# Block-sparse attention followed by an FFN: row-tiled scores, a mask product on VectorE, channels-first AV, row sums on TensorE, and operands turned by transposing DMAs

## Chip, cores, metric

The kernel runs on one core of one Trainium2 chip. The metric is device microseconds (us) of one execution; a kernel's figure is the median of its runs. A run can fall into a slower state, with a lower granted clock (the share of full speed that TensorE's clock was allowed, as the trace records it) and a longer time. A profile is of one run; those of e1 and e9 are of runs 1.8 and 2.0 us above their medians, that of e3 of one 3.6 above, that of e6 of its fastest. A profiled execution lists the span from the first to the last instruction, which is about 2 us shorter than the execution's time.

## The reference

```python
# q, k, v: (4 batches, 8 heads, 768 positions, 64) float32
scores = (q @ k.transpose(0, 1, 3, 2)) / sqrt(64)
mask   = window of +-1 block of 32 | first/last block row/column | 3 sampled blocks per block row
attn   = softmax(where(mask, scores, -1e9))
x      = (attn @ v) as 3072 tokens x 512 channels
h      = x @ w_in                            # 512 -> 2048
out    = (h * sigmoid(beta * h)) @ w_out     # 2048 -> 512, float32
```

Both kernels compute all 768x768 scores of each head densely in fp16 with float32 accumulation and apply the mask to them. They use sigmoid(z) = (1 + tanh(z/2))/2, and no maximum is subtracted before exp.

## The kernel before

Two heads form a *pair*, of 128 channels. k, q and v of a pair are loaded as float32, cast on VectorE, turned by TensorE (`tp`) and evicted by VectorE into operands of up to 128 rows: 64 channels plus 24 rows (one for each block of 32 positions) that carry the mask as a product of block one-hots, so that one matmul gives masked scores. The FFN of a group of tokens is kept in a backlog of small pieces that are put between the attention steps of the next group.

```python
def emit_prep(b, j):                                   # cut
    for name, st32 in (("k", kst), ("q", qst)):
        nc.vector.tensor_copy(out=st16..., in_=st32...)          # cast
        for c in range(NC):                                      # NC = 6
            nc.tensor.transpose(out=tp[:, c, :], in_=st16[:, c, :, :]..., identity=identity)
        nc.vector.tensor_copy(out=four[f"{name}A"][0:D, :], in_=flat[0:D, :])
        nc.vector.tensor_copy(out=four[f"{name}B"][D:P, :], in_=flat[D:P, :])
    ...                                                # v is cast into va, beside a column of ones

def step(hh, kc0):                                     # scores of one head, cut
    for i in range(kn):
        nc.tensor.matmul(sc[:, i * n:(i + 1) * n],
                         lhsT=kx[0:rows, (kc0 + i) * P:(kc0 + i + 1) * P],   # rows = 88 or 128
                         rhs=qx[0:rows, q0:q0 + n], start=True, stop=True)
    nc.scalar.activation(out=et[:, 0:kn * n], in_=sc[:, 0:kn * n], func=AF.Exp, scale=SCALE)

def av_step(hh):                                       # tokens first, cut
    for qc in range(nq):
        for kc in range(NC):
            nc.tensor.matmul(av[:, qc, :], lhsT=et[...128 columns...],
                             rhs=va[:, hh, kc, 0:D + 1],         # 65th column: the row sum
                             start=(kc == 0), stop=(kc == NC - 1))
    nc.vector.reciprocal(out=recip[:, 0:nq], in_=av[:, 0:nq, D])
    nc.vector.tensor_tensor(out=xstage..., in0=av..., in1=recip..., op=ALU.mult)
    if hh == 1:
        ...                                            # xtp: turned by TensorE, evicted into xT_sb

def h_step(f):                                         # FFN, cut; both kernels have it
    for c in range(NPAIR):
        nc.tensor.matmul(hp[:, 0:n], lhsT=w_in_sb[:, c, f * P:(f + 1) * P], rhs=xT_sb[...], ...)
    nc.scalar.activation(out=t_sb, in_=hp, func=AF.Tanh, scale=beta_h_sb[:, f:f + 1])
    nc.vector.scalar_tensor_tensor(out=g[:, f, 0:n], in0=t_sb, scalar=1.0, in1=hp, ...)
def o_step(ts, quarter):
    ...                                                # 4 of 16 matmuls of op; after the last: osb, store
```

The softmax here doesn't subtract the row's maximum and nothing guards it: scores larger than these inputs give would overflow.

## Time and profile before

| before | |
|---|---|
| time | 339.36 us, median of 3 (339.35 to 339.81) |
| span of the profiled execution | 337.4 us |
| busy: TensorE (PE), ScalarE (ACT), VectorE (DVE) | 298.4, 215.8, 181.7 us |
| first score, first FFN matmul (hp), last score | 21.7, 52.7, 313.4 us |

The profile page first gives each engine's busy time, then the span in 40 equal slices with the busy share in tenths, then the chain of work that ended last, by engine. These are those lines of the page of the kernel before.

```profile
PE 298.4 (88%) x2659; PEld 172.2 (51%) x2659; DVE 181.7 (54%) x408; ACT 215.8 (64%) x297; POOL 28.0 (8%) x48
...
PE   0055589999999999999999999999999999999995
...
DMA  7999994112530340021340000011000010001101
...
PE 64%; DVE 16%; ACT 14%; issue 4%; DMA 2%; SPq 0%; ACTq 0%; DVEq 0%
```

After six slices (50 us) TensorE is busy nearly without a break, and the DMA engines, full at first, are idle most of the time. What bounds this kernel is the stream of matmuls, plus a start of about 50 us.

Groups of the page: line, engine, operation, output<-inputs, shape, count | busy us, mean ns of one | idle before, and what ended it.

```profile
L240 ACT ACTIVATE et<-sc 128x1024 f16<-128x1024 f32 (+1 forms) x160 | 146.8, 953 | 80.4 <-PE sc L234 80.2
L313 PE MATMUL op<-w_out_sb,g 128*128 128x512 f16 x384 | 97.0, 379 | 0.1
```

ScalarE waits 80 us for scores, so it is not the limit; `op` waits for nothing. The mean of 379 ns is a matmul from start to modelled end; from start to start one takes 216 ns.

**An account of TensorE's time.** I use one account for every kernel, worked out from the start times of the matmuls in the trace. Each matmul is charged its columns at 0.417 ns; tiles that run side by side are counted once ("stream"). Where the trace's record of the granted clock is 0.5 (half speed), and before its first record, where the spacings are twice as long as well, the extra time of the stream is put under "half clock". A gap of up to 150 ns between matmuls of different kinds is "change of kind", a longer one is a wait for whatever the trace names as having ended it. What remains is "other": waits for g or for transposes on TensorE, and some 3 ns per matmul. The expectations quoted below were written with an earlier form of it, in which the half clock was not kept apart and counted from other starting points, so their figures differ by some us from those here.

### The profile page before, as it was taken

How to read it: one execution, taken by the hardware profiler on the slowest of the kernel's cores; microseconds unless marked ns; L12 is line 12 of the kernel's file. 1: busy time of each engine (PE TensorE's matmuls, PEld its weight loads, DVE VectorE, ACT ScalarE, POOL GpSimd, SP SyncE). 2: the span in 40 equal slices, each digit the busy share in tenths (PEclk: the TensorE clock that was granted, in tenths of full speed). 3: DMA queues.
4: the chain of work that ended last, by engine and by line, in shares of the span. 5: the costliest groups of instructions: out<-in, count | busy, mean ns of one | idle time of the engine just before them, and what ended most of it. 6: DMA issues, size and time to landing. Idle time of an engine off the chain costs nothing.

```text
span 337.4 us, 6399 instructions
## 1 busy us (share of the span) xinstructions
PE 298.4 (88%) x2659; PEld 172.2 (51%) x2659; DVE 181.7 (54%) x408; ACT 215.8 (64%) x297; POOL 28.0 (8%) x48
## 2 busy tenths in 40 slices
PE   0055589999999999999999999999999999999995
PEld 0034466655555555555566445455455455555662
DVE  3989764543787451557866366115667114561360
ACT  1011389985998545978554989665986756954561
POOL 9994000000000000000000000000000000000000
PEclk9999999999999999999999999999999999999999
DMA  7999994112530340021340000011000010001101
GB/s 242 384 228 225 267 330 179 50 47 80 161 97 11 123 130 33 31 79 64 96 157 31 33 0 2 31 38 58 1 3 0 33 62 33 0 2 62 64 2 62
DMA packets 20880, 29.78 MB, mean 88 GB/s; under 512 B 1380, under 2 KB 17780, under 8 KB 20852
## 3 DMA queue, kind: packets, MB, share of 16 engines
q1 hardware_dynamic: 16512, 25.17, 21.8%
q0 software_dynamic: 4224, 4.19, 7.5%
q8 instruction: 21, 0.34, 0.4%
q14 instruction: 7, 0.06, 0.1%
q10 hardware_dynamic: 116, 0.01, 0.0%
HBM read 27.27 MB, written 6.29 MB: 99 GB/s over the span
## 4 chain that ended last, share of the span: by engine, by line
PE 64%; DVE 16%; ACT 14%; issue 4%; DMA 2%; SPq 0%; ACTq 0%; DVEq 0%
PE op L313 23%; PE hp L294 16%; PE sc L234 12%; PE av L260 9%; ACT et L240 8%; ACT t_sb L299 6%; DVE g L301 4%; PE tp L209 2%; PE xtp L274 2%; DMA qst<-in_q_dram 2%; DVE q_203 L204 1%; DVE va_70 L217 0%; DVE xst L266 0%; DVE qB_157 L214 0%; DVE qB_139 L214 0%
## 5 line engine op out<-in xcount | busy, mean ns | idle before, releaser
L240 ACT ACTIVATE et<-sc 128x1024 f16<-128x1024 f32 (+1 forms) x160 | 146.8, 953 | 80.4 <-PE sc L234 80.2
L313 PE MATMUL op<-w_out_sb,g 128*128 128x512 f16 x384 | 97.0, 379 | 0.1
L294 PE MATMUL hp<-xT_sb,w_in_sb 128*128 128x512 f16 (+1 forms) x448 | 95.6, 348 | 1.0 <-DVE g L301 0.2
L301 DVE SCALAR_TENSOR_TENSOR g<-t_sb,hp 128x512 f16<-128x512 f16 (+1 forms) x112 | 67.1, 610 | 44.9 <-ACT t_sb L299 44.4
L299 ACT ACTIVATE t_sb<-hp,beta_h_sb 128x512 f16<-128x512 f32 (+1 forms) x112 | 69.8, 653 | 12.1 <-PE hp L294 10.9
L294 PEld LDWEIGHTS <-w_in_sb 128*128 128x128 f16 x448 | 42.2, 97 | 35.9 <-issue 1.9
L260 PEld LDWEIGHTS <-et 128*128 128x128 f16 x1152 | 44.2, 99 | 21.6 <-DVE xst L266 10.4
L313 PEld LDWEIGHTS <-g 128*128 128x128 f16 x384 | 34.9, 97 | 33.2 <-DVE qB_163 L214 0.4
L265 DVE RECIPROCAL recip<-av 128x2 f32<-128x2 f32 (+1 forms) x64 | 11.2, 176 | 70.3 <-PE av L260 70.0
L318 ACT ACTIVATE osb<-op 128x512 f32<-128x512 f32 x24 | 14.3, 598 | 23.2 <-PE op L313 19.7
L266 DVE TENSOR_TENSOR xst<-av,recip 128x128 f16<-128x128 f32 (+1 forms) x64 | 22.8, 357 | 1.6
L276 DVE COPY xT_sb<-xtp 128x256 f16<-128x256 f16 (+1 forms) x32 | 11.5, 358 | 14.6 <-PE xtp L274 14.6
L274 PEld LDWEIGHTS <-xst 128*128 128x128 f16 x96 | 6.4, 97 | 12.5 <-DVE xst L266 12.2
L260 PE MATMUL av<-va_70,et 128*128 128x65 f16 x216 | 9.6, 199 | 2.8 <-DVE xst L266 2.7
L234 PE MATMUL sc<-qB_139,kB_138 128*128 128x256 f16 (+1 forms) x48 | 11.6, 344 | 0.5 <-ACT et L240 0.5
L274 PE MATMUL xtp<-identity,xst 128*128 128x128 f16 x96 | 10.9, 222 | 1.0 <-DVE xst L266 0.9
L234 PE MATMUL sc<-qA_137,kA_136 88*128 88x256 f16 (+1 forms) x48 | 11.1, 344 | 0.5 <-ACT et L240 0.3
L180 PE MATMUL mkx<-onehot,mask_121 24*24 24x512 f16 (+1 forms) x2 | 0.8, 506 | 10.3 <-DVE mask_121 L126 10.3
L260 PE MATMUL av<-va_72,et 128*128 128x65 f16 x216 | 9.5, 196 | 0.0
L234 PE MATMUL sc<-qB_145,kB_144 128*128 128x256 f16 (+1 forms) x36 | 8.8, 348 | 0.9 <-ACT et L240 0.9
L234 PE MATMUL sc<-qA_143,kA_142 88*128 88x256 f16 (+1 forms) x36 | 8.7, 350 | 0.6 <-ACT et L240 0.6
L234 PE MATMUL sc<-qB_163,kB_162 128*128 128x512 f16 (+1 forms) x36 | 8.5, 325 | 0.7 <-ACT et L240 0.7
(206 smaller groups left out, 249.4 us busy)
## 6 DMA issues: line engine op xcount, KB each, us to landing
kst<-in_k_dram SPq DMA_DIRECT2D x16, 384.0 KB, 4.7
qst<-in_q_dram SPq DMA_DIRECT2D x16, 384.0 KB, 5.5
vst<-in_v_dram SPq DMA_DIRECT2D x16, 384.0 KB, 5.4
out_dram<-osb SPq DMA_DIRECT2D x24, 256.0 KB, 2.0
w_in_sb<-in_moe_w_in_dram POOLq DMA_DIRECT2D x4, 512.0 KB, 10.1
w_out_sb<-in_moe_w_out_dram POOLq DMA_DIRECT2D x4, 512.0 KB, 21.7
sb_i_95<-in_sampled_blocks_dram ACTq DMA_DIRECT2D x1, 0.3 KB
beta_sb<-in_moe_beta_dram ACTq DMA_DIRECT2D x1, 8.0 KB, 4.5
```

Source lines behind the costliest of these rows:

```text
L234: nc.tensor.matmul(sc[:, i * n:(i + 1) * n], lhsT=kx[0:rows, (kc0 + i) * P:(kc0 + i + 1) * P], rhs=qx[0:rows, q0:q0 + n], start=True, stop ...
L240: nc.scalar.activation(out=et[:, 0:kn * n], in_=sc[:, 0:kn * n], func=AF.Exp, bias=0.0, scale=SCALE)
L260: nc.tensor.matmul(av[:, qc, :], lhsT=et[:, i * n + qc * P:i * n + (qc + 1) * P], rhs=va[:, hh, kc, 0:D + 1], start=(kc == 0), stop=(kc == ...
L265: nc.vector.reciprocal(out=recip[:, 0:nq], in_=av[:, 0:nq, D])
L266: nc.vector.tensor_tensor(out=xstage[:, 0:nq, hh * D:(hh + 1) * D], in0=av[:, 0:nq, 0:D], in1=recip[:, 0:nq].to_broadcast([P, nq, D]), op= ...
L274: nc.tensor.transpose(out=xtp[:, qc, :], in_=xstage[:, qc, :], identity=identity)
L276: nc.vector.tensor_copy(out=xT_sb[:, j, b * S + q0:b * S + q0 + n], in_=xtp[:, 0:nq, :].rearrange("p c s -> p (c s)"))
L294: nc.tensor.matmul(hp[:, 0:n], lhsT=w_in_sb[:, c, f * P:(f + 1) * P], rhs=xT_sb[:, c, t0:t0 + n], start=(c == 0), stop=(c == NPAIR - 1))
L299: nc.scalar.activation(out=t_sb[:, 0:n], in_=hp[:, 0:n], func=AF.Tanh, bias=0.0, scale=beta_h_sb[:, f:f + 1])
L301: nc.vector.scalar_tensor_tensor(out=g[:, f, 0:n], in0=t_sb[:, 0:n], scalar=1.0, in1=hp[:, 0:n], op0=ALU.add, op1=ALU.mult)
L313: nc.tensor.matmul(op, lhsT=g[:, f, ts * P:(ts + 1) * P], rhs=w_out_sb[:, f, :], start=(f == 0), stop=(f == N_FFC - 1))
L318: nc.scalar.activation(out=osb, in_=op, func=AF.Copy, bias=0.0, scale=0.5)
```

## The change

The intent is to take work off TensorE, which bounds the kernel.

- The scores of even and odd chunks of 128 keys run side by side in two row tiles of 64 rows (a row or column tile is a part of TensorE's 128x128 array that works on a matmul of its own; the way the array is cut is the tiling mode); the mask becomes a product with a 0/1 mask after exp, on VectorE.
- AV gives channels first (V as weights, exp moving), so that `xtp` and its eviction go; two heads run side by side in column tiles. Row sums become matmuls with ones, four tiles side by side. The reciprocal goes through DRAM and comes back spread over 64 partitions.
- k, q, v are cast by the loads (on GpSimd's queue) and turned by transposing DMAs (on SyncE's queue), so that `tp`, the casts and evictions go.
- The program order is fixed by hand, with lags in steps; `osb` moves from ScalarE to VectorE.

The core of the diff; setup, mask building, and the parts that only move are cut:

```diff
+    ctx.enter_context(tc.manual_schedule())
...
+    def emit_load(i):
+        for src, dst in ((k, k_stage[i % NST]), (q, q_stage[i % NST][:, 1:2 * NC + 1, :]), (v, va...)):
+            nc.gpsimd.dma_start(out=dst..., in_=src[b, 2 * j:2 * j + 2]...)       # casts to fp16
+    def emit_turn(i):
+        nc.sync.dma_start_transpose(out=kT, in_=k16.rearrange("p c d -> p (c d)"))
+        nc.sync.dma_start_transpose(out=qT[:, 1:2 * NC + 1:2, :], in_=q16[:, 1:2 * NC + 1, :]...)
+        nc.sync.dma_start_transpose(out=qT[:, 0:2 * NC + 1:2, :], in_=q16...)
...
-        nc.tensor.matmul(sc[:, i * n:(i + 1) * n], lhsT=kx[0:rows, ...], rhs=qx[0:rows, q0:q0 + n], ...)
+                for i, (hh, g) in enumerate(pieces):
+                    for par in range(2):
+                        nc.tensor.matmul(sc[:, par, i, :],
+                            lhsT=kT[par * D:(par + 1) * D, hh * (NC // 2) + g, :],
+                            rhs=qT[par * D:(par + 1) * D, lo:lo + nq, :], start=True, stop=True)
                 nc.scalar.activation(out=et, in_=sc, func=AF.Exp, bias=0.0, scale=SCALE)
+                nc.vector.tensor_tensor(out=et, in0=et, in1=mask_pg[...], op=ALU.mult)
...
+        def sums():
+            dt = av_pool.tile([P, 512], FP32, tag="av", name="dsum")     # av_pool has one buffer
+            ... for t in range(4):
+                    nc.tensor.matmul(dt[32 * t:32 * t + 32, 0:256],
+                        lhsT=sel[:, h, :] if nh == 2 else ones32,
+                        rhs=ets[(t // 2, t % 2, kc)][:, h * 256:(h + 1) * 256], ...)
+            nc.vector.reciprocal(out=r[...], in_=dt[...])                # twice, 128 columns
+            nc.sync.dma_start(out=dr, in_=r)                             # to DRAM
+            ... nc.sync.dma_start(out=rb[hh * D:(hh + 1) * D, 0:n], in_=src.to_broadcast([D, n]))
+        def av(jj):
+            at = av_pool.tile([P, 512], FP32, tag="av", name="av")
+            for kc in range(NC):
+                for hh in range(2):
+                    nc.tensor.matmul(at[hh * D:(hh + 1) * D, 0:n], lhsT=va[:, hh, kc, :],
+                                     rhs=ets[(jj, hh, kc)], ...)
+            nc.vector.tensor_tensor(out=xt[...], in0=at[:, 0:n], in1=box["rb"][jj][:, 0:n], op=ALU.mult)
...
+    for i in range(1, NPAIR):
+        emit_load(i)
+    for i in range(4):
+        emit_w_in(i)
+    for i in range(4):
+        emit_w_out(i)
+    LAG_S, LAG_A0, LAG_A1 = 2, 8, 9          # steps from a couple's last score to sums, av, av
+    PACE = 1.28                              # us of FFN work fed behind each score step
+    ... while n_turned < len(seq) and first_use[n_turned] <= x + 7: emit_turn(n_turned) ...
+        feed(PACE if x < n_steps else 1.0)
```

Steps are 144, one exp of 128x1024 each; a *couple* is two pairs of one block of 256 or 512 queries.

## The prediction

> **What bounds it now.** TensorE. Busy: PE 298 us of 337, ACT 216, DVE 182; the chain of waits is 64% PE. Start-to-start spacing in the timeline: 216 ns for a 512-column matmul (op: 32 in 6.92 us), about 39 ns for a 65-column av matmul. With these the PE stream is: hp 83, op 83, scores 62, av 45, transposes (tp, xtp) about 18 us, 291 in all. The rest is the start: windows show PE busy only 12.6 of the first 40 us (first exp at 22.6, FFN from about 50 us), and a tail of about 5 us. So 291 + about 40 = 337.
>
> **What the change does.**
> - Scores: K=64 in two row tiles, 384 matmuls; if pairs run side by side, 62 becomes 31 us.
> - AV: weights V (64 columns, two column tiles), moving exp; 31 us instead of 45, and no xtp.
> - Row sums: 576 new matmuls of 256 columns in four column tiles; 16 us if four truly run at once, more likely 22 to 28 (576 at av's 39 ns is 22).
> - tp and xtp go (-18); mask 1 us. PE stream: 291 to about 253.
> - The matmul order has 272 changes of tiling mode. The Trainium skill, TensorEngine Tiling (Array Packing), Key Properties, says that changing the mode drains TensorE; this trace has nothing to size it. I put 0.06 us each: 16 us. PE then is about 269.
> - DVE loses the prep casts and evictions, xst and xT, gains 160 mask products. The skill, VectorE: DVE Perf Modes, tier table, gives tensor_tensor on 16-bit SBUF data the 2x mode; estimate 0.65 us per 1024 columns, 95 us. Reciprocals become 32 of 128 columns: the trace has 170 ns for 2 and 182 for 4 columns, so about 0.9 us each, 30 us. Output eviction moves from ACT (0.6 us x 24). DVE about 235 us.
> - ACT: 144 exps at 0.95 spacing plus tanh 70: about 215, as before.
> - DMA: 48 transposes and 32 small DRAM round trips on one queue; about 19 MB of casting loads. No limit on average; the first scores need three loads, then three transposes: first exp at 14 to 18 us, first steps paced by transposes that share the engines with weights.
>
> **Critical path.** FFN work waits for step 22 of 144, which I expect at about 43 us. After it PE still has about 243 us plus drains. In the h half of each 512-token group the sums per engine are nearly equal (PE 20+, ACT 21, DVE 21 us), so ACT and DVE stall PE there: I allow 10 us in all, also for sums and av sharing one PSUM bank. With the tail: 43 + 259 + 10 - overlap of a few + 5, a gain of about 30 us.
>
> Predicted **309 us**, range 286 to 334; faster by over 2% 0.81, within 2% 0.11, slower 0.08.
>
> **What would show it.** Score pairs starting almost together, 216 ns per pair; av pairs likewise; sums about 110 to 170 ns per four; gaps of some 60 ns at changes of mode; mask products 0.6 to 0.7 us; reciprocals about 0.9 us; PE idle after 45 us waiting mostly for ACT and DVE in h phases.
>
> **What would make it wrong.** Tiles that do not overlap (scores, av and sums would then cost up to 100 us more: slower). Mask product in 1x mode[...]. Slow transposes (over 5 us each) or their queue blocked behind round trips and stores. Switches of mode much dearer than 0.06 us, or free (then about 293).

## More of the kernel before

The timeline (start us, length us, engine, line, work) of a stretch of the kernel before:

```profile
146.39 1.02 PE L294 MATMUL hp<-xT_sb,w_in_sb 128*128 128x512 f16 x4
147.25 0.54 PE L260 MATMUL av<-va_80,et 128*128 128x65 f16 x12
147.63 0.82 PE L234 MATMUL sc<-qB_145,kB_144 128*128 128x256 f16 x6
```

Four hp matmuls take 0.86 us up to the start of the av behind them, four times 216 ns: going from one kind of matmul to another costs nothing here. The trace gives all of them the form 128\*128, half of the scores 88\*128.

## The result, and the profile after

The changed kernel takes **391.27 us**, median of 4 (386.89 to 391.70), against 339.36 (339.29 to 339.81) before: ratio 1.150, 95% interval 1.144 to 1.155, slower. The result is correct. (A ratio is the mean time of one kernel's fast runs over that of the other's of the same rounds, so not quite the ratio of the medians quoted.)

The same lines of the page of the changed kernel:

```profile
PE 300.1 (77%) x2189; PEld 129.4 (33%) x2189; DVE 226.5 (58%) x390; ACT 206.8 (53%) x261; POOL 41.1 (11%) x63
...
PE   2410132689973999997797898999999998889995
...
DMA  8999999300698951159596310191552013100201
...
PE 49%; DMA 17%; ACT 15%; DVE 13%; issue 5%; POOL 1%; SPq 0%; DVEq 0%; POOLq 0%; ACTq 0%
```

The busy 300.1 us of PE hide that the work has shrunk, which the account below, made from start times, shows. What the slices show is the start: TensorE is nearly idle in the first six (58 us), where the DMA engines are full, and gets going after eight (78 us). DMA is now 17% of the chain that ended last. The groups that answer to the question of cost:

```profile
L221 DVE TENSOR_TENSOR et<-et,mask 128x1024 f16<-128x1024 f16 (+1 forms) x128 | 78.3, 623 | 54.5 <-ACT et L214 54.2
L208 PE MATMUL sc<-qT,kT 64*128 64x256 f16 (+1 forms) x384 | 60.5, 361 | 51.6 <-DMA qT<-q 42.2
...
L313 PE MATMUL op<-w_out_sb,g 128*128 128x512 f16 x384 | 91.9, 381 | 0.0
...
L245 DVE RECIPROCAL recip<-dsum 128x128 f32<-128x128 f32 x32 | 28.2, 924 | 7.2 <-PE dsum L238 7.2
```

The mask products and the reciprocals cost what was predicted. The scores waited 42.2 us for `qT`, which is new: in the kernel before, TensorE turned them itself. SyncE's timeline shows how long it was held by each transpose, early on and later:

```profile
17.17 5.41 SPq L92 DMA_TRANSPOSE qT<-q  x1
22.63 5.66 SPq L95 DMA_TRANSPOSE qT<-q  x1
28.40 4.73 SPq L91 DMA_TRANSPOSE kT<-k  x1
33.23 4.83 SPq L92 DMA_TRANSPOSE qT<-q  x1
38.15 6.35 SPq L95 DMA_TRANSPOSE qT<-q  x1
...
101.70 1.24 SPq L91 DMA_TRANSPOSE kT<-k  x1
103.04 1.23 SPq L92 DMA_TRANSPOSE qT<-q  x1
```

The same transpose holds the queue for 1.24 us at 102 us and for about four to five times that at 17 to 44 us. The view of the DMA queues says why; from 20 to 30 us it gives, per queue, packets, MB and share of the engines' time, and for each issue the median us to landing:

```profile
q0 software_dynamic: 1631, 1.55, 92.2%
q1 hardware_dynamic: 1632, 0.40, 31.0%
...
qT<-q SPq DMA_TRANSPOSE x2, 16.0
```

q0 carries the casting loads and the weights (GpSimd's queue), q1 the transposes. They take turns packet by packet, 1631 against 1632, and a transpose's packet is 256 bytes where nearly all of q0's are of 768 or 1024. The Trainium skill, DMA: Bandwidth & Descriptors, "Queues, rings and completion order", says that a DMA engine round-robins between queue rows at packet granularity; the even counts of this trace agree. So in this stretch the queue with small packets gets a fifth of the bytes (0.40 of 1.95 MB), however urgent it is. A transpose of q issued here lands 16 us after its issue; from 101 to 106 us, 3.3 us after.

Then TensorE in the steady part, from its timeline:

```profile
104.28 1.90 PE L313 MATMUL op<-w_out_sb,g 128*128 128x512 f16 x8
106.11 0.39 PE L208 MATMUL sc<-qT,kT 64*128 64x512 f16 x2
106.43 1.49 PE L269 MATMUL av<-et,va 128*64 128x512 f16 x12
107.85 1.04 PE L313 MATMUL op<-w_out_sb,g 128*128 128x512 f16 x4
```

Eight op matmuls take 1.83 us up to the start of the score behind them, 0.10 us more than eight times 216 ns. A score pair takes 0.32 us up to the av behind it instead of 0.22. The skill, TensorEngine Tiling (Array Packing), "Key Properties", says that changing the tiling mode drains TensorE; the trace agrees in that each such change adds 0.10 us, though it doesn't show what fills that time. The 12 av matmuls are six pairs side by side, 1.42 us with one change in it. So the tiles do run together, and a change of mode has a price.

What ended TensorE's waits from 86 us on (engine, line, releaser: us in total, times, longest):

```profile
PE dsum L238 <- DVE xt L273: 8.1, 6, 1.9
PE av L269 <- DVE xt L273: 7.6, 6, 5.2
PE av L269 <- DVE recip L245: 5.1, 5, 1.6
PE sc L208 <- ACT et L214: 4.4, 7, 0.9
```

dsum and av share one PSUM bank: each waits until VectorE has read the one before it. And xt needs `rb`, which comes through DRAM; the wait of 5.2 us is for an rb that came late. Last, the clock. Windows of the changed kernel (window; us; then busy us and counts of PE, PEld, DVE, ACT, POOL; then granted clock, DMA share, GB/s):

```profile
173.00:176.50 3.50, 2.77 (x22) 1.10 (x21) 2.90 (x6) 2.05 (x2) 0.68 (x1) 1.00 1.00 243
176.50:179.90 3.40, 1.46 (x32) 0.92 (x33) 2.46 (x4) 1.02 (x1) 0.74 (x2) 1.00 1.08 183
179.90:183.30 3.40, 3.40 (x18) 1.21 (x15) 0.80 (x2) 0.57 (x1) 0.00 (x0) 0.50 1.41 156
```

A window in which waits left PE 1.46 us of work in 3.40 us is followed by one at half clock, 3.4 us long. The two other half-clock stretches between the first hp and the last matmul also follow such windows (busy 0.2 and 1.45 us). The skill, TensorE: Matmul & The Clock Gate, Part 1, tells of a gate that halves the clock after an idle window of about 3.4 us; the lengths (3.4 and 6.8 us in this kernel) agree, though TensorE was not wholly idle in the windows here. The start of both kernels agrees too: until the first record of the full clock, at 42.8 us before and 84.3 us after, a 256-column score matmul of the kernel before took 213 ns from start to start, later 109.

The account for all kernels that the argument uses, in us of the profiled execution; everything right of "first hp" counts from there on:

| | span | first hp | stream | changes (number) | half clock | waits xt + recip | waits exp | waits qT | other |
|---|---|---|---|---|---|---|---|---|---|
| before | 337.4 | 52.7 | 258.6 | 2.9 (358) | 0.0 | – | 5.0 | – | 14.2 |
| after | 389.9 | 85.7 | 233.4 | 23.8 (237) | 5.3 | 24.1 | 5.6 | 0 | 7.8 |
| e1 | 367.7 | 64.2 | 233.2 | 24.1 (239) | 7.9 | 21.6 | 5.4 | 0 | 7.3 |
| e2 | 382.4 | 84.3 | 232.9 | 23.7 (236) | 7.4 | 8.1 | 5.4 | 8.6 | 7.8 |
| e3 | 397.6 | 89.2 | 232.8 | 14.8 (149) | 11.1 | 28.5 | 5.6 | 0 | 11.4 |
| e5 | 366.3 | 59.1 | 233.0 | 23.8 (237) | 8.8 | 10.9 | 5.2 | 12.0 | 7.8 |
| e7 | 350.8 | 52.4 | 233.4 | 23.7 (236) | 4.5 | 19.0 | 5.6 | 0 | 8.0 |
| e9 | 353.9 | 60.1 | 233.2 | 20.3 (204) | 5.3 | 18.3 | 5.6 | 0 | 7.0 |
| e10 | 358.4 | 57.0 | 233.1 | 20.3 (204) | 5.2 | 25.8 | 5.6 | 0 | 7.3 |
| e11 | 383.0 | 59.0 | 245.5 | 24.3 (252) | 4.4 | 23.6 | 3.7 | 0 | 18.5 |
| e12 | 357.3 | 55.2 | 245.4 | 24.6 (254) | 1.4 | 6.7 | 4.4 | 0 | 15.6 |
| e13 | 357.1 | 55.0 | 245.2 | 21.3 (219) | 3.0 | 8.9 | 4.1 | 0 | 15.4 |

The row's parts and the span differ by 4 to 6 us, the time after the last matmul. Read the first two rows: the stream behind the first hp fell by 25 us, as intended; changes of kind gave back 21, waits for the one PSUM bank and the reciprocal 24, the half clock 5, and the FFN began 33 us later. What is left over ("other") fell by 6. Together that is the loss of 52 us.

### The profile page after: what moved, and what is told of

It is laid out like the page before. It is cut to its first block, busy times and chain, and to the rows that moved or that the text cites. A ratio compares the mean times of both kernels' runs of the same rounds, so it can differ in the third digit from the quotient of the medians.

```text
span 389.9 us, 5616 instructions
## 1 busy us (share of the span) xinstructions
PE 300.1 (77%) x2189; PEld 129.4 (33%) x2189; DVE 226.5 (58%) x390; ACT 206.8 (53%) x261; POOL 41.1 (11%) x63
## 4 chain that ended last, share of the span: by engine, by line
PE 49%; DMA 17%; ACT 15%; DVE 13%; issue 5%; POOL 1%; SPq 0%; DVEq 0%; POOLq 0%; ACTq 0%
PE op L313 21%; DMA qT<-q 12%; PE hp L292 10%; ACT et L214 10%; PE av L269 6%; PE sc L208 6%; ACT t_sb L297 5%; PE dsum L238 4%; DVE recip L245 4%; DMA dr<-recip 3%; DMA rb<-dr 3%; DVE g L299 2%; DVE xt L273 2%; DVE et L221 2%; DVE osb L318 1%
## 5 line engine op out<-in xcount | busy, mean ns | idle before, releaser
L214 ACT ACTIVATE et<-sc 128x1024 f16<-128x1024 f32 x144 | 145.5, 1031 | 123.6 <-PE sc L208 123.5
L221 DVE TENSOR_TENSOR et<-et,mask 128x1024 f16<-128x1024 f16 (+1 forms) x128 | 78.3, 623 | 54.5 <-ACT et L214 54.2
L208 PE MATMUL sc<-qT,kT 64*128 64x256 f16 (+1 forms) x384 | 60.5, 361 | 51.6 <-DMA qT<-q 42.2
L292 PE MATMUL hp<-xt,w_in_sb 128*128 128x512 f16 (+1 forms) x448 | 95.7, 353 | 2.0 <-DVE g L299 1.3
L292 PEld LDWEIGHTS <-w_in_sb 128*128 128x128 f16 x448 | 39.7, 98 | 45.2 <-issue 18.2
L269 PE MATMUL av<-et,va 128*64 128x256 f16 (+1 forms) x384 | 42.7, 363 | 14.5 <-DVE xt L273 8.0
L208 PEld LDWEIGHTS <-kT 64*128 64x128 f16 x384 | 16.9, 98 | 108.4 <-issue 107.7
L217 DVE TENSOR_TENSOR et<-et,mask 128x1024 f16<-128x1024 f16 x32 | 22.0, 688 | 52.4 <-ACT et L214 52.1
L269 PEld LDWEIGHTS <-va 128*64 128x64 f16 x384 | 22.5, 118 | 30.6 <-issue 23.1
L245 DVE RECIPROCAL recip<-dsum 128x128 f32<-128x128 f32 x32 | 28.2, 924 | 7.2 <-PE dsum L238 7.2
L318 DVE TENSOR_SCALAR osb<-op 128x512 f32<-128x512 f32 x24 | 16.5, 688 | 15.9 <-PE op L313 15.6
L273 DVE TENSOR_TENSOR xt<-av,rb 128x256 f16<-128x256 f32 (+1 forms) x32 | 17.7, 553 | 13.4 <-PE av L269 8.4
L82 POOL DMA_DIRECT2D k<-in_k_dram x16 | 11.7, 732 | 105.0 <-DMA kT<-k 96.2
L82 POOL DMA_DIRECT2D q<-in_q_dram x16 | 11.6, 725 | 26.5 <-DMA qT<-q 21.3
## 6 DMA issues: line engine op xcount, KB each, us to landing
w_out_sb<-in_moe_w_out_dram POOLq DMA_DIRECT2D x4, 512.0 KB, 23.7
```

Source lines behind the costliest of these rows:

```text
L82: nc.gpsimd.dma_start(out=dst.rearrange("p (h c) d -> p h (c d)", h=2), in_=src[b, 2 * j:2 * j + 2].rearrange("h (p c) d -> p h (c d)", c=NC))
L208: nc.tensor.matmul(sc[:, par, i, :], lhsT=kT[par * D:(par + 1) * D, hh * (NC // 2) + g, :], rhs=qT[par * D:(par + 1) * D, lo:lo + nq, :], ...
L214: nc.scalar.activation(out=et, in_=sc, func=AF.Exp, bias=0.0, scale=SCALE)
L221: nc.vector.tensor_tensor(out=et[:, :, i, :], in0=et[:, :, i, :], in1=mask_pg[:, :, g, q0:q0 + n], op=ALU.mult)
L245: nc.vector.reciprocal(out=r[:, x * 128:(x + 1) * 128], in_=dt[:, x * 128:(x + 1) * 128])
L269: nc.tensor.matmul(at[hh * D:(hh + 1) * D, 0:n], lhsT=va[:, hh, kc, :], rhs=ets[(jj, hh, kc)], start=(kc == 0), stop=(kc == NC - 1))
```

## The experiments

All give the correct result except e7. The kernel before took 339.4 to 339.6 us (medians) beside them. Each is an edit of the changed kernel ("after").

### e1: weights behind the first transposes

The theory: the start is late because the transposes share the DMA engines with the weights. The weight loads now wait until the twelve transposes of the first batch have landed.

```diff
-    for i in range(4): emit_w_in(i)
-    for i in range(4): emit_w_out(i)
...
+    for i in range(NPAIR): emit_turn(i)
+    nc.gpsimd.tensor_copy(out=w_in_sb[0:1, 0, 0:1], in_=kq[seq[3]][1][0:1, 0, 0:1])   # waits for qT
+    for i in range(4): emit_w_in(i)
+    for i in range(4): emit_w_out(i)
+    (two loads of the next batch)
```

> The eight weight loads are issued only after the twelve transposes of the first four head pairs have landed; nothing else changes. Theory A (the transposes, 256-byte packets, share each DMA engine packet by packet with the casting loads, so weight traffic stretches them from about 1.3 to 4-6 us): in the first 25 us as before, then the other transposes at about 1.3 us each; last of the twelve issued by about 35 us instead of 56; first hp matmul at 50 to 58 us instead of 86; time 355 to 368 us. Rival B (a transpose between SBUF tiles costs 4 us in itself, or the loads of the head pairs alone do it): transposes stay at 4 to 6 us, first hp at 80 us or later, and since the weights also come later, 391 to 420 us.

Measured: 367.69 us (365.88 to 371.02), ratio 1.085 [1.078, 1.092], 24 us less than after. SyncE's timeline of e1:

```profile
22.82 1.21 SPq L91 DMA_TRANSPOSE kT<-k  x1
24.13 1.23 SPq L92 DMA_TRANSPOSE qT<-q  x1
...
29.45 1.25 SPq L95 DMA_TRANSPOSE qT<-q  x1
34.55 0.36 SPq L248 DMA_DIRECT2D dr<-recip  x1
40.37 2.45 SPq L255 DMA_DIRECT2D rb<-dr  x4
```

The transposes now take 1.2 us each once the loads are in; TensorE's waits for qT fell from 42.2 us to 9.3. (The three just before, from 13.3 us on, beside the casting loads but not the weights, held the queue for 3.91, 3.52 and 1.88 us: the loads alone slow transposes too.) The first hp came at 64 us, though, later than the range expected. The weights now collide with the next small transfers: `dr`, issued at 34.55, landed at 40.36, and `rb` at 45 to 49 us. TensorE waited 8.3 us in one place for the xt that needs it. The theory holds for the transposes; the round trip through DRAM suffers the same.

### e2: AV two steps later

```diff
-    LAG_S, LAG_A0, LAG_A1 = 2, 8, 9
+    LAG_S, LAG_A0, LAG_A1 = 2, 10, 11
```

> The two AV steps of a couple come 10 and 11 steps after its last score instead of 8 and 9, so that in 256-query tiles they no longer stand beside the sums of the next couple, with which they share one PSUM bank, and the reciprocals' way through DRAM has two steps more. Theory A (these waits of TensorE, 24 us after 86 us in the trace, are on the critical path): the waits of dsum and av for xt, recip and the late rb fall below 6 us, time 368 to 378 us. Rival B (TensorE is not what binds there; ACT or DVE are, or the delay comes back at the end as two more steps before the last FFN): waits fall but the time stays within 386 to 394.

Measured: 383.94 us (383.38 to 385.73), 1.132 [1.129, 1.136]. Waits for xt and recip fell by 16 us behind the first hp, yet the time fell by only 7, a miss: it lies between the ranges of theory and rival. The waits of e2 from 84 us on show what took the rest:

```profile
PE sc L208 <- DMA qT<-q: 8.3, 2, 6.2
PE av L269 <- DVE xt L273: 5.6, 10, 1.1
```

Two new waits for transposes, late in the kernel, where earlier there had been slack. So the waits were real and partly hid the next ones; the half clock also rose by 2.1 us.

### e3: FFN pieces at every second step only

This halves the changes of tiling mode at the same work.

```diff
-        feed(PACE if x < n_steps else 1.0)
+        if x >= n_steps: feed(1.0)
+        elif x % 2: feed(2 * PACE)
```

> FFN work is given out after every second score step, twice as much at a time: about half of the 181 changes between row-tiled scores and full matmuls go. Theory A (each change costs TensorE about 0.096 us, seen as 312 instead of 216 ns after a 512-column matmul, and TensorE binds from 86 us on): about 85 changes less, 8 us less, 380 to 385 us. Rival B (the 0.1 us is hidden by waits on other engines): 388 to 394. Rival C (bigger bursts of hp wait for their three PSUM tiles): slower than 394, with new waits of hp on g.

Measured: 395.78 us (394.51 to 399.43), 1.168 [1.162, 1.174], slower than after. The account shows 88 changes and 9.0 us of them gone, and more than that come back: half clock +5.8, waits for xt and recip +4.4, other (mostly waits for g) +3.6, first hp +3.5. That larger pieces block the engines for longer is my reading; no run separates it. The profile is of the slowest run of the four.

### e4: w_in in one DMA with rows four times as long (one look)

If packets alternate, larger packets on the other queue must make the transposes slower.

```diff
-        nc.gpsimd.dma_start(out=w_in_sb[:, :, i * 512:(i + 1) * 512],
-                            in_=w_in_r[:, :, i * 512:(i + 1) * 512])
+        nc.gpsimd.dma_start(out=w_in_sb[:, :, :], in_=w_in_r[:, :, :])
```

> w_in is loaded by one DMA with rows of 2048 columns instead of four of 512: the same bytes in a quarter of the packets, each four times as long. Theory A (queues alternate packet by packet): a transpose that falls into the w_in load takes about four times as long there as before, 15 us or more instead of 5; w_in itself still takes 12 to 14 us. Rival B (queues share bandwidth by bytes, or the transposes are slow for another reason): transposes stay at 4 to 6 us. One look only; the time is not judged, within 380 to 400 by both.

Measured: 395.68 us, one run. SyncE's timeline of e4:

```profile
13.73 8.69 SPq L91 DMA_TRANSPOSE kT<-k  x1
22.47 14.67 SPq L92 DMA_TRANSPOSE qT<-q  x1
37.18 5.33 SPq L95 DMA_TRANSPOSE qT<-q  x1
```

14.67 us for a transpose while w_in moves, and 5.33 for the next one, during which w_in landed (at 39.6 us). The view of e4's DMA queues from 24 to 31 us:

```profile
q0 software_dynamic: 366, 1.15, 98.0%
q1 hardware_dynamic: 364, 0.09, 17.5%
```

The weights' packets had become 4096 bytes and took 322 ns each (median) instead of 96, and the counts of packets were again even. With e1, that settles the cause of the slow transposes. (w_in itself landed 28 us after its issue, not in the 12 to 14 expected; in the changed kernel its four parts took from 12.2 to 36.6 us.)

### e5: e1 and e2 together, and stores on GpSimd's queue

```diff
 (e1 and e2)
-                    nc.sync.dma_start(out=rows[s0 // P], in_=osb)
+                    nc.gpsimd.dma_start(out=rows[s0 // P], in_=osb)
```

> Weights late and AV two steps later together, and the output stores are issued by GpSimd instead of the queue that also issues transposes and round trips. If the losses are separate and additive (theory A): 391 less 23.5 (weights) less 7.4 (AV later), and the new waits of scores for qT that AV later brought (8.6 us at 127 and 203 us) go, since a transpose no longer stands behind a store that waits for its FFN: 347 to 354 us, waits for qT after 60 us below 1 us. Rival B (the transposes were late for the DRAM round trips in the queue, not for the stores): waits for qT stay at 5 us or more, 355 to 362.

Measured: 369.52 us (368.07 to 369.81), 1.089 [1.087, 1.091], no better than e1 and outside both ranges expected. The account has e1's start and e2's lower bank waits, but 12 us of waits for qT from mid-kernel. GpSimd's and SyncE's timelines of e5:

```profile
141.12 0.56 POOL L322 DMA_DIRECT2D out_dram<-osb  x1 [4.39 <-DVE osb L318]
141.68 0.72 POOL L82 DMA_DIRECT2D k<-in_k_dram  x1
```

```profile
145.17 5.67 SPq L92 DMA_TRANSPOSE qT<-q  x1
...
154.62 5.88 SPq L91 DMA_TRANSPOSE kT<-k  x1
```

A store waits in order for its osb, the loads of later pairs queue up behind it and come in bursts, and the transposes slow down beside them. Moving the stores was a mistake of mine, as it seems (e9 moves them back, but changes the lead of the transposes with it); it showed that the collision can be made anywhere in the kernel.

### e6: e5, and pieces of op at every second step

```diff
-        feed(PACE if x < n_steps else 1.0)
+        if x < n_steps and x % 2 == 0 and backlog and backlog[0][0] == 0.86:
+            feed.left += PACE
+        else:
+            feed(PACE if x < n_steps else 1.0)
```

> As e5, and in the output-projection half of each group (op matmuls only, which wait for no PSUM tile of ACT's) the FFN work is given out at every second step. Theory A (a change of tiling mode costs TensorE 0.1 us on the critical path; the halved switches failed before only because of bursts of hp): some 40 to 50 changes less, no new waits of hp on g, 3.5 to 5 us less than e5. Rival B (the time of a change is hidden elsewhere): the same as e5 within 1.5 us, the count of changes down all the same.

Measured: 365.46 us, median of three fast runs (364.34 to 368.73; a fourth, slow, took 369.94), 1.079 [1.073, 1.085], 4 us less than e5 and with an interval clear of e5's. Changes fell from 237 to 199 and by 3.8 us, which fits theory A. But single runs of e5 and e6 still overlap, and in the profiles from the first hp on waits for qT fell too, from 11.7 to 9.1 us, while those for xt rose from 8.4 to 10.8. So what the changes alone gave is not shown.

### e7: e1 without the round trip of the reciprocal (wrong result)

```diff
-            dr = dram_pool.tile(...); nc.sync.dma_start(out=dr, in_=r)
-            ... rb loaded from dr ...
+            box["rb"] = [fake_rb, fake_rb]        # a constant tile
```

> As weights late, but AV is multiplied by a constant, so nothing waits for the reciprocals' way through DRAM (sums and reciprocals still run; the result is wrong on purpose). Theory A (with the weights late, this way collides with them: waits of dsum and av for xt of 8.6, 4.4 and 3.3 us): first hp at 49 to 54 us instead of 64, and 350 to 355 us instead of 367.7. Rival B (first hp is then bound by w_in itself or the scores): first hp not before 60, gain below 6 us.

Measured: 352.67 us (351.83 to 353.35), 1.039 [1.037, 1.041]: 15 us less than e1, of which the first hp, at 52.4 us as in the kernel before, gives 12. So the round trip costs e1 15 us, most of it at the start, where weights are moving. The 19 us of waits for xt and recip that stay are those for the shared bank alone, since nothing waits for rb any more.

### e8: e6 at a slower feed of the FFN

```diff
-    PACE = 1.28
+    PACE = 1.18
```

> As e6, FFN given out at 1.18 instead of 1.28 us per step, so that a group's FFN lasts 23.4 of its 24 steps and fewer steps have scores alone, where TensorE waits for exp (8.5 us before 86 us and 5.6 us after it in the changed kernel). Theory A: these waits halve after 60 us, 2 to 4 us less than e6. Rival B (what is not done in the steps comes back at the end as FFN alone): same as e6 or up to 4 us more.

Measured: 365.67 us (364.02 to 367.77), 1.078, within the spread of e6's fast runs. Waits for exp over the whole kernel went from 9.2 to 8.3 us, those for qT from 18.4 to 25.5. No gain shown, and theory A's halving of the waits for exp did not come.

### e9: e1, e2, e6's pairing and e8's pace; stores back on SyncE, transposes up to 12 steps ahead

```diff
-        while n_turned < len(seq) and first_use[n_turned] <= x + 7:
+        while n_turned < len(seq) and first_use[n_turned] <= x + 12:
```

> As e8, but the output stores go back to the queue of the transposes, and each transpose is issued up to 12 steps ahead of its first use instead of 7. Theory A (after the start, the scores wait for qT because prefetching loads run beside the transposes, packet by packet, in e5 because loads were held up behind stores on GpSimd and came in a bunch; more lead hides it): waits for qT after 60 us below 2 us instead of 10 to 17, time 350 to 357. Rival B (the queue's order alone, whatever the lead): 5 us or more of such waits stay, 358 or more.

Measured: 353.68 us (352.38 to 355.71), 1.042 [1.038, 1.046], the best correct version. The waits of e9 from 60 us on:

```profile
PE av L269 <- DVE xt L273: 15.1, 12, 4.7
PE sc L208 <- ACT et L214: 4.4, 7, 0.9
```

No wait for qT is left there. Its long waits for xt (3.0 us at 85, 4.7 at 106) are waits for rb beside loads.

### e10: e9, and w_out only after the second couple's reciprocal has come back

```diff
+                if x == 14:
+                    nc.gpsimd.tensor_copy(out=w_out_sb[0:1, 0, 0:1], in_=rb_last[0][0:1, 0:1])
+                    (the four loads of w_out, two loads of the next batch)
```

> As e9, and the four w_out loads are issued only when the second couple's reciprocals have come back from DRAM. Theory A (the way through DRAM of the first couples is slow because of the weight packets on the same engines): the second couple's way takes under 6 us instead of 10 to 12, first hp at 54 to 57 us instead of 59, 1 to 5 us less than e9. Rival B (w_in alone already makes the wait, or w_out is then late for the first op): same as e9 or slower.

Measured: 359.31 us (358.21 to 360.33), 1.058, slower than e9. The first hp came 3 us sooner, at 57.0, and one wait for xt of 13 us appeared, ending at 91 us: a later reciprocal was issued at 77 us, behind transposes that moved beside the postponed loads, and its rb landed from 89 us on. The collision was moved, not taken away.

### e11: the changed kernel with TensorE turning k and q again

```diff
-        nc.sync.dma_start_transpose(out=kT, ...)   (three of them)
+        for dst, src, nn in ((kT[:, 0:NC, :], kf, NC), (qT[:, 1:2 * NC + 1:2, :], qf[:, D:...], NC),
+                             (qT[:, 0:2 * NC + 1:2, :], qf, NC + 1)):
+            tp = mm_pool.tile([P, NC + 1, P], FP16, tag="mm", name="tp")
+            for c in range(nn):
+                nc.tensor.transpose(out=tp[:, c, :], in_=src[:, c * P:(c + 1) * P], identity=identity)
+            nc.vector.tensor_copy(out=dst, in_=tp[:, 0:nn, :])
```

(At the start one pair is turned at once instead of two, the next three at most two steps ahead of their use instead of seven.)

> The changed kernel with one part undone: the chunk pairs are turned by TensorE (19 transposes of 128x128 for each head pair) and copied out of PSUM by VectorE, no transpose DMAs; weights, AV and stores as in the changed kernel. It costs TensorE 16 x 19 x 56 ns, 17 us, and VectorE about 16 x 2.4 us, 38 us. Theory A (the transposes' starvation behind the loads made the start): first scores before 15 us, the fourth pair's scores before 32 us instead of 65, first hp at 46 to 56 us instead of 86, and although 13 us of TensorE work more are left after the start, 362 to 374 us. Rival B (the start is bound by the sheer bytes of loads and weights, or by the way through DRAM): first hp not before 70 us, 385 us or more.

Measured: 384.76 us (382.45 to 385.63), 1.132, only 6.5 us less than after, a miss. The first hp came 27 us sooner, at 59.0. The stream behind it is 12 us longer, and so are other waits, by 11 (for g and for PSUM buffers of the transposes). The rest of its start is the round trip under the weights: a wait for xt of 8.4 us that ends at 45 us.

### e12: e11 with AV two steps later

> As e11 with AV two steps later (as e2). Waits for qT cannot come back here, so if the bank waits are on the critical path the gain over e11 is larger than e2's 7 us: 10 to 15 us, 350 to 362 us. If VectorE, now with about 265 us of work, has become the bound, the gain is below 5 us. Neither is expected to beat the kernel before (339).

(The edit is e2's on top of e11.) Measured: 358.79 us (357.55 to 359.69), 1.056 [1.054, 1.059], 26 us less than e11; I had expected less. The waits of e12 from 55 us on:

```profile
PE av L275 <- DVE xt L279: 4.7, 7, 1.1
PE sc L214 <- ACT et L220: 3.3, 6, 0.9
```

Waits for xt and recip fell by 17 us behind the first hp, nearly what e2 took away, but here nothing came in their place: with no transposing DMA there is no wait for qT to uncover (8.6 us in e2), the half clock fell by 3.0, where in e2 it rose by 2.1, and the first hp came 3.8 sooner. Together they are 24 us of the 26.

### e13: e12 with pieces of op at every second step

> As e12 (no transpose DMAs, AV later), with op work given out at every second step. In e12 the account of TensorE has about 256 changes of tiling mode of 0.097 us, 24.8 us, and no waits for qT that could blur the comparison as in e6. Theory A (the changes are on the critical path): 35 to 50 changes less, so 3 to 5 us less than e12's 358.8, ratio to before 1.042 to 1.048. Rival B (a change fills time that TensorE would wait anyway): the count falls, the time stays within 1 us of e12, ratio 1.054 to 1.058.

(The edit is e6's.) Measured: 358.43 us (357.89 to 358.84), 1.055 [1.053, 1.057], the same as e12. Its waits from 55 us on:

```profile
PE av L275 <- DVE xt L279: 6.5, 8, 1.7
```

Changes fell by 35 and 3.3 us; waits for xt and recip rose by 2.2, the half clock by 1.6. As in e3, what left as changes of mode came back as waits and half clock.

### e14: e13 with the slower feed

> As e13 with FFN at 1.18 us per step. Theory A (fewer steps with scores alone, less bunching of g on VectorE): the waits of hp and of the transposes on g (4.7 us after 60 us in e12) and on exp (4.4 us) fall by half, 2 to 5 us less than e13. Rival B: within 1.5 us of e13. Not expected to beat before: 24.8 us of changes less the 4 saved stand against 11 us of stream saved.

(The edit is e8's.) Measured: 361.64 us, median of five fast runs (359.21 to 362.09; a sixth, slow, took 366.77), 1.063 [1.060, 1.066]: no gain, but 3 us slower than e13. No cause was looked for.

No version was faster than the kernel before.

## Why the prediction was wrong

The forecast can be laid beside the account term by term. It read 43 (start) + 243 (stream) + 16 (changes) + 10 (waits) + 5 (tail) less 8 for "overlap of a few" = 309. The trace of the changed kernel has 85.7 + 237.6 + 23.8 + 33.3 + 5.3 + 4.2 = 389.9; here the 4.2 us of fixed cost per matmul are moved from "other" to the stream, where the prediction's 216 ns had them, 33.3 is 24.1 + 5.6 + the remaining 3.6 of other, and 5.3 is the half clock.

1. **The start, 43 against 85.7: the step that failed.** The prediction had "first steps paced by transposes that share the engines with weights" and "No limit on average", and still put the FFN's first work "at about 43 us". It knew of the sharing and gave it no price. Shown: packets alternate (1631 to 1632), transposes take 4 to 6 us instead of 1.24, larger packets on the other queue make it 14.67 (e4), and with the weights out of the way the first hp is nearly 22 us sooner (e1). The second half is the reciprocal's trip through DRAM, which e7 prices at 15 us in e1, 12 of them before the first hp. Without either, in e7, the first hp still came at 52.4 us, not at 43. Of these last 9 us, 5 to 9 lie before the first exp, forecast "at 14 to 18 us": it came at 23.3 in e7 and 23.6 in the changed kernel, after a wait for qT of over 8 us, while the transposes ran beside the casting loads; with TensorE turning k and q (e11) it came at 18.2. It listed "Slow transposes (over 5 us each)" among what would make it wrong, which is what came.
2. **Waits behind the start, "I allow 10 us in all", against 33.3.** It named engines' equal loads and the one PSUM bank. exp costs 5.6 us, as in the kernel before (5.0). The bank, and the rb that must come first, cost 24.1; e2 and e12 show 16 and 17 us of them to go with two more steps of lag, and e7 that 19 do not need a late rb.
3. **Changes of mode, 0.06 us each, against 0.10.** 237 seen ones cost 23.8 us; the mechanism was right and the size short by 8 us. That removing 35 or 88 of them (e13, e3) shortens the kernel by as much is not shown: in e3 and e13 the time came back as waits and half clock. So whether 23.8 us is what they cost on the critical path is left open.
4. **The half clock, not in the prediction, 5.3 us** after the first hp. Each stretch of it follows a window in which waits left TensorE busy less than half (0.2, 1.46 and 1.45 of 3.4 us), so it looks like a price on top of the waits. That is read from the trace; no run was made to test it.
5. **"Overlap of a few", 8 us, had nothing to stand for.** The other terms are stretches of one engine's time, and such stretches cannot overlap.
6. **What was right.** Score pairs and av pairs run side by side (the second of a pair starts about 4 ns after the first, median): the stream behind the first hp fell by 25 us and came out 5 us below the forecast. That nearness is in part luck: the row sums ran four at once (109 ns for four, 15.4 us in all), where it had allowed 22 to 28 us; and its 39 ns for an av matmul of the kernel before is not what the trace shows, which is 32 ns from start to start at full clock, so that its 45 us for that kernel's av, and the gain on av, were some 8 us too high. The mask product takes 0.69 us per 1024 columns. The skill, VectorE: DVE Perf Modes, "The perf-mode tier table", gives the 2x mode, and the trace agrees with the estimate of 0.65 us. Reciprocals take 0.92 us, VectorE is busy 226 us (about 235 forecast), ScalarE 207.

So the gain on the bounding engine was delivered, 25 us, and then paid away: to changes of mode and the bank, and most of all to a start in which small packets on one queue compete with large ones on the other.

What stays open: what a change of mode costs on the critical path (e6 may speak for the full price, e3 and e13 against it); and whether a second PSUM bank for av (the pools hold 4 + 1 + 3 banks as they are; no run gave av another) would free the 19 us of bank waits without a longer lag.

## What to carry to other kernels

Before moving work from a busy engine to DMA, look at what else moves at that time: small packets on an urgent queue beside large ones on another got a small share of the bytes here (0.40 of 1.95 MB), so order the urgent small transfers before the bulk ones, and look for every further small transfer (here the reciprocal's round trip) that the bulk will then meet. Price the start by itself, from the first load to the first bulk matmul, for it can outweigh a gain in the stream. A wait that goes can uncover the next one (16 us gone and 7 gained in e2), so judge a fix by the whole account of the engine and not by the wait that vanished.

## What the Trainium skill lacked or had wrong

- TensorEngine Tiling (Array Packing), "Key Properties": it says that a change of mode drains TensorE but gives no figure. Here it was 0.10 us per change (23.8 us for 237), against 0.008 us between kinds of full-array matmuls (2.9 us for 358).
- Advanced Engine Details and Errata, "X-Bar Transpose (TRN2)": it calls transposing DMAs as fast as regular ones, with 350 to 400 GB/s expected. Here, with nothing beside it, one of 196,608 bytes (every third 229,376) was issued each 1.33 us (e1, 22.8 to 29.5 us), 156 GB/s worked out, in packets of 256 bytes, with the DMA engines busy 78% of the time (24 to 31 us); beside casting loads and weights one of 196,608 bytes took 4.7 to 5.4 us, which is 36 to 42 GB/s. No run here tells whether its issue or its movement set the 1.33 us.
- DMA: Bandwidth & Descriptors, "Queues, rings and completion order": the arbitration it states was seen (1631 to 1632 packets), but not its consequence, that the bytes a queue gets go with its packet size: 0.40 MB against 1.55 MB in 10 us, and a transpose of 14.67 us when the other queue's packets were 4096 bytes.
- TensorE: Matmul & The Clock Gate, Part 1: it speaks of idle windows, and of frequent short idling between groups of matmuls, but gives no busy share at which the clock falls. Here two windows of 3.4 us in which TensorE was busy 1.46 and 1.45 us were each followed by one at half clock.
